# RWKV-7 and a GELU MLP on one core: one TensorE product replaced by block transposes on VectorE, and the first MLP product run in 64x64 tiles

## The chip, the core and the metric

The kernel runs on one core of a Trainium2 chip. The metric is the device time of one execution in microseconds. A core has a matrix engine (TensorE, PE in the profile), VectorE (DVE), ScalarE (ACT), GpSimd (POOL) and SyncE (SP), which here only issues DMAs. Each engine takes its instructions in order, and they wait for each other by semaphores.

## The reference

Everything is in 32-bit floats. A recurrence over 768 tokens runs for 4 batches of 8 heads of dimension 40; its output goes through an MLP of 320 to 2048 to 320 with exact GELU on 3072 tokens.

```python
for t in range(S):
    y[:, :, t] = np.einsum('bhd,bhde->bhe', rt, state)
    Sa = np.einsum('bhde,bhe->bhd', state, at)
    state_decay = state * wt[:, :, None, :] - np.einsum('bhd,bhe->bhde', Sa, bt)
    state = state_decay + np.einsum('bhd,bhe->bhde', vt, kt)
...
h = x @ w_in
g = 0.5 * h * (1.0 + erf(h * inv_sqrt2))
return (g @ w_out)
```

## The kernel before

The tokens are cut into 12 chunks of 64. Within a chunk the recurrence is written as matrix products: the scaled a and b give N (products a.b below the diagonal), whose inverse is needed; k and a give A, v and r give RV. All these 64x64 blocks, one for each of 32 batch-head pairs, are made by `products` (L577) in TensorE tiles of 64 rows by 64 columns, and masked to the upper triangle by VectorE (`masked`, L574).

What a chunk c does, in the order of the loop at L1257:

- `corner` and `joined` (L775, L790) complete the inverse (Tt) from its 32x32 diagonal blocks, with two 32x32 products (J and J2 in the trace). L, which J reads, is Tt turned by VectorE (`turn_corner`).
- `make_X` multiplies the state by a (X) and adds what A and v give (av): xs.
- `make_sa` (L822) multiplies Tt and xs to sa by tokens (tile sap, copied into SM by `copy`); `make_saT` (L834) computes the same product the other way round (saT_ps, copied into saT by two ScalarE copies). So the chunk has sa in both orientations: saT is needed for the product M with r, and sa, which stands beside the masked M in the tile SM, for the last product.
- `make_y2` multiplies r by the turned state into the PSUM tiles QY, `make_M` makes M and masks it into SM, and `make_QY` adds b.SM and k.VR (VR holds v and the masked RV). `outputs` scales QY to the MLP's input xt and to the new state st. `turn_blocks` turns the new state in sixteen 32x32 block steps on VectorE (tile turned).

The inverse of the diagonal blocks is computed two chunks ahead: N is stored to DRAM by SP (`make_N`), read back in another layout (Nb), worked column by column on GpSimd in 62 instructions (L672, L674), stored from GpSimd's queue (inv), and fetched by SP as Tt and T2. The inputs of chunk c+2 are loaded and prepared within chunk c: a, b, k, v and r are read as pairs of rows and turned by VectorE (L186), and the decay w gives the scales wp, en and rw.

The MLP fills TensorE's time. `mlp(c)` (L998) is a generator; each `fill()` in the loop runs it to its next `yield`. A piece of the first product (tile ph) is 20 matmuls of 64x128 weights and 256 columns, in two row tiles side by side, followed by a GELU on ScalarE into gt. From chunk 3 on the second product is computed by `seven` (L947), a seven-product scheme over 2x2 blocks (tile po), whose sums and differences of gt VectorE makes (s1, s2 and the changed blocks of gt). In the steady loop four pieces of ph stand behind X, J2, saT and M of the next chunk, and the po products between the QY pair and the next J.

The order on every engine is the order in which the program issues its instructions (the schedule is manual). PSUM tiles come from a ring of four (`duo`), which is shared by the products and the MLP.

Of the kernel before, what the change touches and what calls it, by code (L numbers as in the profile page):

```python
# [19 lines left out]
def kernel(  # L20
# [464 lines left out]
    def scale_b(c):  # L485
        rwv, wp = decays[c]
        nb = padded[:, c % 2] if c < NB else b_rows[c % 2]
        to = nb[:, :, :, :D] if c < NB else rows(nb)
        nc.vector.scalar_tensor_tensor(to, raws.pop((c, "b")), -1.0, rwv, ALU.mult, ALU.mult)
        turned_in[c]["nb"] = nb  # L490
# [41 lines left out]
    def turn_k(c):  # L532
        t = turned_in[c]
        if c >= NB:
            kT = by_batch(side("k_turned", "conv", 2))
            turn(kT, c, "k_turned")
            en = t.pop("en")
            nc.vector.tensor_tensor(en, kT, en, ALU.mult)
            t["kT"] = parts_by_batch(en)
# [3 lines left out]
        t["kT"] = parts(kT)  # L543

# [80 lines left out]
    def mask_RV(c):  # L625
        t = turned_in[c]
        masked(flat(t["VR"])[:, :, D:], t.pop("RV_ps"))
# [162 lines left out]
    def joined(c):  # L790
# [11 lines left out]
        for q, copy in ((0, nc.scalar.copy), (1, nc.scalar.copy if 0 < c < NS else nc.vector.tensor_copy)):  # L802
# [31 lines left out]
    def make_saT(c):  # L834
# [8 lines left out]
        nc.scalar.copy(to[:, :, 0::3], pt[:, 0])  # L843
        nc.scalar.copy(to[:, :, 1:3], pt[:, 1])
        t["saT"] = parts(saT)

# [24 lines left out]
    def make_QY(c):  # L871
        t = turned_in[c]
        for n, (l_, r_) in enumerate(((t["nb"], t["SM"]), (t["ks"], t["VR"]))):
# [124 lines left out]
    def mlp(c):  # L998
        xt = xts.pop(c)
        for q in range(NF // 4):  # L1000
            ph = duo("ph").rearrange("p x (s t) -> p x s t", s=2)
            for s in range(2):
                p = 2 * q + s
                for kt in range(NK):
                    for x in range(2):
                        nc.tensor.matmul(ph[:, x, s], w_in_sb[half(x), kt, p * P:(p + 1) * P], xt[half(x), kt],  # L1006
                                         start=kt == 0, stop=kt == NK - 1)
            nc.scalar.activation(gt[:, 4 * q:4 * q + 4].rearrange("p (x s) t -> p x s t", x=2), ph, ACT.Gelu)  # L1008
            if c >= NS and q == NF // 4 - 1:
                s1, s2 = half_tile("conv", 2), None  # L1010
                nc.vector.tensor_tensor(s1, block(1, 0), block(1, 1), ALU.add)  # L1011
                if c >= NCH - 2:
                    s2 = half_tile("conv", 2)
                    nc.vector.tensor_tensor(s2, s1, block(0, 0), ALU.subtract)
            yield
        if c >= NS:
            yield from seven(c, s1, s2)
# [239 lines left out]
    for c in range(2, NCH):  # L1257
        n, n2 = c + 1, c + 2
        more, more2 = n < NCH, n2 < NCH
        corner(c)  # L1260
        make_X(c)
        if c > 2:
            turn_blocks(range(4, 16))
        if c == NS + 1:
            weight_sums(3)
        if c == 2:
# [8 lines left out]
            load_v(n)  # L1275
        else:
# [108 lines left out]
```

## Time and profile before

| | us |
|---|---|
| median of three runs | 705.4 (704.87 to 706.5) |
| the profiled execution's own time | 706.29 |
| span of its trace, first to last instruction | 704.3 |
| one period of the chunk loop (J to J) | 49.31 |

In the profile each 32-bit matmul is two records, so 40 records of ph are the 20 matmuls of a piece. PEld is the weight load, which runs beside other matmuls. A row of a timeline gives the start, the duration of the merged group, the engine, line, operation, written and read tiles, shapes and count, and in brackets how long the engine stood idle before it and who released it. SPq rows are DMAs being issued on SP's queue: their duration is that of the issue, not of the transfer.

### The profile page before, as it was taken

The numbers are of one execution on the slowest core, as the hardware profiler recorded it, in microseconds if no ns is written. First come the engines' busy times: TensorE is split into PE (matmuls) and PEld (weight loads), VectorE is DVE, ScalarE is ACT, GpSimd is POOL, SyncE is SP. The second block draws the span as 40 slices with busy tenths as digits, with TensorE's granted clock in tenths as the row PEclk, the third lists the DMA queues.
The fourth block names the chain that finished last, engine by engine and source line by source line (L and its number), as shares of the span: only waits on it lengthen the run. The fifth ranks groups of instructions, "written<-read, shape, count | busy, mean of one in ns | idle before, by whom it ended". The sixth has DMA issues, their size and how long they took to land.

```text
span 704.3 us, 32679 instructions
## 1 busy us (share of the span) xinstructions
PE 662.4 (94%) x14706; PEld 580.0 (82%) x14706; DVE 431.8 (61%) x633; ACT 214.4 (30%) x299; POOL 332.8 (47%) x790
## 2 busy tenths in 40 slices
PE   7588897779999999999999999999999999999997
PEld 4577777657777877889899898998898898998987
DVE  2324889975255666669579488587686694562303
ACT  5124674444131330340341241332323403112020
POOL 5384458810860850871852853835827708600000
PEclk9675799879999999999999999999999999999999
DMA  9688537764665765765666747747758652120100
GB/s 129 120 170 154 103 88 199 136 115 99 118 129 94 125 125 88 130 122 98 125 119 120 140 89 129 139 83 141 138 93 148 126 101 55 37 40 3 35 6 19
DMA packets 287923, 74.45 MB, mean 106 GB/s; under 512 B 265736, under 2 KB 284456, under 8 KB 287784
## 3 DMA queue, kind: packets, MB, share of 16 engines
q1 hardware_dynamic: 283360, 68.20, 52.1%
q0 software_dynamic: 864, 2.36, 2.1%
q8 instruction: 115, 1.88, 1.1%
q10 hardware_dynamic: 3560, 1.80, 1.0%
q14 instruction: 24, 0.20, 0.1%
HBM read 58.69 MB, written 9.70 MB: 97 GB/s over the span
## 4 chain that ended last, share of the span: by engine, by line
PE 77%; DVE 6%; ACT 2%; issue 1%; DMA 1%; ACTq 1%; SPq 0%; DVEq 0%
PE ph L1006 29%; PE po L959 19%; PE po L1023 7%; PE QY L110 6%; PE J L110 2%; PE X L110 2%; PE av L110 2%; PE sap L110 2%; PE saT_ps L110 1%; PE N_ps L110 1%; PE M_ps L110 1%; PE RV_ps L110 1%; PE A_ps L110 1%; PE wT_ps L110 1%; DVE conv L324 1%
## 5 line engine op out<-in xcount | busy, mean ns | idle before, releaser
L1006 PE MATMUL ph<-xt,w_in_sb 64*128 64x256 f32 x1920 | 219.5, 381 | 0.0
L1006 PEld LDWEIGHTS ph<-xt,w_in_sb 64*128 64x128 f32 x1920 | 182.4, 187 | 22.3 <-issue 0.7
L672 POOL TENSOR_TENSOR tmp<-W,Nb 128x126 f32<-128x126 f32 (+22 forms) x310 | 121.5, 392 | 167.0 <-DMA Nb<-N 143.4
L674 POOL TENSOR_TENSOR W<-W,tmp 128x126 f32<-128x126 f32 (+22 forms) x310 | 129.0, 416 | 24.3
L1008 ACT ACTIVATE gt<-ph 128x1024 f32<-128x1024 f32 x48 | 49.1, 1023 | 152.1 <-PE ph L1006 152.0
L959 PE MATMUL po<-w_out_sb,gt 128*128 128x160 f32 x576 | 84.8, 303 | 0.1
L959 PEld LDWEIGHTS po<-w_out_sb,gt 128*128 128x128 f32 x576 | 78.9, 190 | 5.2 <-issue 3.3
L927 DVE STREAM_TRANSPOSE turned<-st 32x256 f32<-32x256 f32 x144 | 62.4, 433 | 2.1
L1023 PE MATMUL po<-w_out_sb,gt 128*128 128x320 f32 x192 | 55.5, 446 | 0.0
L1023 PEld LDWEIGHTS po<-w_out_sb,gt 128*128 128x128 f32 x192 | 36.7, 195 | 15.3 <-issue 1.3
L787 ACT COPY Js<-J 128x256 f32<-128x256 f32 x11 | 4.1, 370 | 95.4 <-PE J L110 95.4
L186 DVE STREAM_TRANSPOSE aT<-a_pairs 128x1024 f32<-128x1024 f32 x9 | 11.2, 1246 | 35.2 <-DMA a_pairs<-in_a_dram 35.2
L1011 DVE TENSOR_TENSOR half<-gt 128x1024 f32<-128x1024 f32 x9 | 11.2, 1247 | 32.8 <-ACT gt L1008 32.8
L575 DVE TENSOR_TENSOR SM<-M_ps,upper 128x1024 f32<-128x1024 f32 x12 | 14.6, 1218 | 23.6 <-PE M_ps L110 23.6
L959 PE MATMUL po<-extra,half 128*128 128x160 f32 x176 | 26.1, 303 | 0.0
L320 ACT ACTIVATE conv<-conv,rebias 128x320 uint32<-128x320 uint32 (+1 forms) x26 | 16.1, 622 | 29.6 <-DVE conv L319 23.2
L959 PEld LDWEIGHTS po<-extra,half 128*128 128x128 f32 x176 | 24.2, 190 | 0.3
L1008 ACT ACT_TABLE_LOAD x10 | 12.8, 1283 | 36.2 <-PE ph L1006 36.1
L963 DVE TENSOR_TENSOR os<-os,po 128x160 f32<-128x160 f32 x36 | 11.5, 319 | 19.0 <-PE po L959 14.3
L575 DVE TENSOR_TENSOR N<-N_ps,upper 128x1024 f32<-128x1024 f32 x12 | 14.7, 1221 | 13.1 <-PE N_ps L110 13.1
L887 DVE TENSOR_TENSOR xt<-QY,wpT 128x512 f32<-128x512 f32 x24 | 15.5, 686 | 11.0 <-PE QY L110 10.9
L662 POOL MEMSET W<- 128x512 f32 x10 | 5.3, 528 | 33.9 <-DMA inv<-W 33.9
(225 smaller groups left out, 1115.6 us busy)
## 6 DMA issues: line engine op xcount, KB each, us to landing
Nb<-N SPq DMA_DIRECT2D x20, 256.0 KB
VR<-in_v_dram SPq DMA_DIRECT2D x24, 160.0 KB
out_dram<-os SPq DMA_DIRECT2D x48, 80.0 KB
b_rows<-in_b_dram SPq DMA_DIRECT2D x22, 160.0 KB
k_rows<-in_k_dram SPq DMA_DIRECT2D x22, 160.0 KB
N<-N SPq DMA_DIRECT2D x44, 64.0 KB
Tt<-inv SPq DMA_DIRECT2D x44, 64.0 KB
a_pairs<-in_a_dram SPq DMA_DIRECT2D x18, 144.0 KB
```

The lines of the kernel that those rows point to most:

```text
L110: nc.tensor.matmul(o, lhsT, rhs, start=first, stop=True, skip_group_check=True)
L320: nc.scalar.activation(power, power, ACT.Relu, bias=rebias, scale=8.0)
L575: nc.vector.tensor_tensor(to, pt, upper.unsqueeze(1).to_broadcast([P, 2 * G * NP, C]), ALU.mult)
L672: eng.tensor_tensor(t, W[:, :rows, j:j + 1].to_broadcast([P, rows, rest]), Nb[:, j:j + 1, j + 1:].to_broadcast([P, rows, rest]), ALU.mult)
L674: eng.tensor_tensor(W[:, :rows, j + 1:], W[:, :rows, j + 1:], t, ALU.add)
L887: nc.vector.tensor_tensor(xt[:, :NP, g * P:(g + 1) * P].rearrange("p i (e t) -> p i e t", e=2), Y, wp[:, g, :, :, :C], ALU.mult)
L927: nc.vector.transpose(tn[to:to + BL, :, at:at + BL], st[at:at + BL, :, g, d * BL:(d + 1) * BL])
L959: nc.tensor.matmul(po[:, n, :DM // 2], l_[:, f], r_[:, f], start=f == 0, stop=f == NF // 2 - 1)
L963: nc.vector.tensor_tensor(to, one_, other, ALU.add)
L1006: nc.tensor.matmul(ph[:, x, s], w_in_sb[half(x), kt, p * P:(p + 1) * P], xt[half(x), kt], start=kt == 0, stop=kt == NK - 1)
L1008: nc.scalar.activation(gt[:, 4 * q:4 * q + 4].rearrange("p (x s) t -> p x s t", x=2), ph, ACT.Gelu)
L1023: nc.tensor.matmul(po[:, g], gt[:, f, g * P:(g + 1) * P], w_out_sb[:, f], start=f == 0, stop=f == NF - 1)
```

## The change

Six things are changed together.

- From chunk 3 on, `make_sa` isn't called. A new function, `sa_blocks`, writes sa by tokens into SM by sixteen 32x32 block transposes of saT on VectorE, twelve behind `make_saT` and four behind `make_M`. Each handles eight blocks. From chunk 4 on the sign of b moves into the copies of saT (now scaled copies on ScalarE).
- A piece of the first MLP product issues 40 matmuls of 64x64 weights instead of 20 of 64x128, in four tiles of the array.
- From chunk 4 on, b and k are scaled by GpSimd (b without the sign), ahead of the inverse's columns, and RV is masked by a ScalarE copy followed by a GpSimd product instead of one VectorE product. For chunk 4 itself the scaling stays on VectorE.
- The turned k is made a chunk later: its transpose stands before the last four state blocks, its scaling with en behind the v transpose.
- Loads are reordered on SP: a is loaded half a chunk earlier, behind the read of Nb; b and k (by rows) are loaded behind the xt copies instead of behind Nb, and the pairs of k behind Nb instead of before xt. The r transpose moves behind that of b.
- s1 and s2 of `seven` are computed at the next fill instead of directly behind the last GELU, and VectorE's copy of J2 is issued ahead of ScalarE's.

The order of PE's products is unchanged except for sap.

```diff
+    def sa_blocks(c, blocks):
+        t = turned_in[c]
+        if "SM" not in t:
+            t["SM"] = SM_ring()
+        saT = t["saT"].rearrange("p q m e t -> p (q m) (e t)")
+        for n in blocks:
+            d, g, e, z = 1 - n // 8, n // 4 % 2, n // 2 % 2, n % 2
+            to, at = e * HP + z * BL, g * HP + d * BL
+            nc.vector.transpose(t["SM"][to:to + BL, g].rearrange("p q m c -> p (q m) c")[:, :, d * BL:(d + 1) * BL],
+                                saT[at:at + BL, :, to:to + BL])
...
-        nc.scalar.copy(to[:, :, 0::3], pt[:, 0])
-        nc.scalar.copy(to[:, :, 1:3], pt[:, 1])
+        sign = 1.0 if c < NB else -1.0
+        nc.scalar.mul(to[:, :, 0::3], pt[:, 0], sign)
+        nc.scalar.mul(to[:, :, 1:3], pt[:, 1], sign)
...
-                    for x in range(2):
-                        nc.tensor.matmul(ph[:, x, s], w_in_sb[half(x), kt, p * P:(p + 1) * P], xt[half(x), kt],
-                                         start=kt == 0, stop=kt == NK - 1)
+                    for to, end in ((0, HP), (HP, P)):
+                        for x in range(2):
+                            nc.tensor.matmul(ph[to:end, x, s], w_in_sb[half(x), kt, p * P + to:p * P + end],
+                                             xt[half(x), kt], start=kt == 0, stop=kt == NK - 1)
...
     def mask_RV(c):
...
+            nc.scalar.copy(to, t.pop("RV_ps"))
+            nc.gpsimd.tensor_tensor(to, to, upper.unsqueeze(1).to_broadcast([P, 2 * G * NP, C]), ALU.mult)
...
+            if more2:
+                turn_a(n2)
+                fetch_pairs(n2, "b_turned", b, nc.sync, False, paired["a"])
+            if more:
+                turn_k(n)
+            if more2:
+                load_r(n2)
+            turn_blocks(range(12, 16))
+            if c == 3:
+                scale_b(n)
+                scale_k(n, nc.vector)
+            fill()
+            make_saT(c)
+            sa_blocks(c, range(12))
         fill()
         make_y2(c)
         make_M(c)
+        if c > 2:
+            sa_blocks(c, range(12, 16))
         if more:
             turn_v(n)
+            if more2:
+                load_v(n2)
+        if more and c > 2:
+            scale_kT(n)
...
         outputs(c)
+        if more2 and c == 2:
+            turn_r(n2)
+            fetch_pairs(n2, "k_turned", k, nc.sync, False, paired["r"])
+        elif more2:
+            load_kb(n2)
         pieces.append(mlp(c))
...
         if more2:
+            if c > 2:
+                scale_b(n2, nc.gpsimd)
+                scale_k(n2, nc.gpsimd)
             steps = start_inverse(n2, nc.gpsimd)
-            load_kb(n2)
+            if more3:
+                load_a(n3)
+            if c == 2:
+                load_kb(n2)
+            else:
+                fetch_pairs(n2, "k_turned", k, nc.sync, False, paired["r"])
             load_VR(n2)
```

More of the change, by code (lines that the diff above doesn't have):

```diff
@@ L801, in joined @@
                     mm(J[lo[q], 0, n // 2], Js[hi[q], n // 2], F[hi[q], n, BL:])
-        for q, copy in ((0, nc.scalar.copy), (1, nc.scalar.copy if 0 < c < NS else nc.vector.tensor_copy)):
+        copies = (0, nc.scalar.copy), (1, nc.scalar.copy if 0 < c < NS else nc.vector.tensor_copy)
+        for q, copy in copies[::-1] if c > 2 else copies:
             copy(F[lo[q], :, BL:].rearrange("p (n z) t -> p z n t", z=2), J[lo[q]])
```

73 lines of the change are left out of this document (36 added, 37 removed).

## The prediction

> **What bounds the kernel now.** I read the page first, then the busy times over one period of the chunk loop, then the chain of work that ended last, then the timelines of the engines over that period.
>
> ```profile
> PE 662.4 (94%) x14706; PEld 580.0 (82%) x14706; DVE 431.8 (61%) x633; ACT 214.4 (30%) x299; POOL 332.8 (47%) x790
> ...
> PEclk9675799879999999999999999999999999999999
> ...
> PE 77%; DVE 6%; ACT 2%; issue 1%; DMA 1%; ACTq 1%; SPq 0%; DVEq 0%
> ```
>
> TensorE is busy for 94% of the span, at 90% or more of full granted clock from a quarter of it on. The next row is one period (from one J product to the next): length, then busy time and instructions of PE, weight loads, DVE, ACT and POOL, then clock, share of the DMA engines and GB/s.
>
> ```profile
> 477.99:527.30 49.31, 49.31 (x1177) 44.70 (x1176) 35.26 (x52) 14.72 (x21) 28.04 (x67) 1.00 0.66 122
> ```
>
> PE has no gap at all in 49.31 us. So a microsecond taken from PE's stream is a microsecond of the period, until another loop becomes longer than PE's. Within PE, the chain shows what a group costs alone and in company (start, us, what):
>
> ```profile
> 588.24 1.07 PE sap L110 x64
> 589.31 1.01 PE saT_ps L110 x62
> 590.33 4.52 PE ph L1006 x40
> 594.84 1.09 PE QY L110 x64
> 595.93 0.93 PE M_ps L110 x64
> ...
> 601.39 3.01 PE QY L110 x128
> ...
> 667.10 17.47 PE ph L1006 x160
> ```
>
> The reader should see two things. Four pieces of the first MLP product (ph) alone between other tile shapes cost 4 x 4.52 = 18.08; four in one run cost 17.47. With a cost u of a piece and s for entering and leaving the run, u + s = 4.52 and 4u + s = 17.47: u = 4.317, s = 0.20. On the other side, the y2 product (first QY row) costs 1.09 and the M product behind it in the same tile shape, with the same count, 0.93: a run of 64x64 products has s = 0.16. So each run of one tile shape costs some 0.18 beside its work.
>
> **The first MLP product in 64x64 tiles.** A piece issues 40 matmuls (80 records, each with a weight load) in place of 20 (40 records), four tiles side by side in place of two. The streamed columns per tile are the same. Does it stream as fast? The QY pair is the row for four tiles with long streams: 128 records in 3.01, less 0.16, over four tiles are 32 steps of 89.1 ns for 104 columns; a ph step now is 4.317/20 = 215.8 ns for 256 columns. Per column that is 0.856 against 0.843 ns.
>
> ```profile
> 460.59 0.74 PE L110 MATMUL cum<-w_tile,cum_m 64*64 64x320 f32 x8
> ...
> 477.99 0.75 PE L110 MATMUL J<-L,N 32*32 32x32 f32 x64
> ...
> 502.61 1.66 PE L110 MATMUL QY<-SM,b_rows 64*64 64x104 f32 x64
> ...
> 518.56 1.16 PE L110 MATMUL N_ps<-aT,nT 40*64 40x64 f32 x64
> ...
> 527.30 0.75 PE L110 MATMUL J<-L,N 32*32 32x32 f32 x64
> ```
>
> The cum row (eight records of 320 columns) confirms four at once: two steps of 320 x 0.843 = 270 ns and a run's 0.2 are 0.74, its duration; with two tiles at a time it would be 1.28. So a piece costs between 4.27 (0.834 ns a column, the slope between the two steps, with nothing fixed) and 4.38 (0.856 x 256). I take 4.32, no change, since that slope with a fixed 2.3 ns fits both rows; the ends are -2 and +3 us over 48 pieces.
>
> The gain is in the runs. From X to QY the loop has the runs X, ph, J2, ph, sap+saT, ph, y2+M, ph, QY: nine. In 64x64 tiles all but J2 (32x32) have one shape and merge: X+ph, J2, and everything behind it: three. Six runs less by 0.18 are 1.08 a chunk, 9.7 over chunks 3 to 11. Chunk 2 (N, ph, sap+saT, ph to one run, ph, y2+M, ph, QY to one) loses six as well: 1.1. Chunks 0 and 1 I count at nothing, because there DVE holds the path:
>
> ```profile
> 114.98 2.36 PE L110 MATMUL QY<-SM,extra 64*64 64x104 f32 x64 [3.60 <-DVE SM L575]
> ```
>
> **sap removed.** Chunks 3 to 11 lose 32 matmuls each: 1.07 less the run's 0.16 is 0.91, nine times 8.2. PE's period becomes 49.31 - 1.08 - 0.91 = 47.32.
>
> **What takes its place on DVE.** Sixteen 32x32 block transposes of saT into SM, of the form of the state's:
>
> ```profile
> 480.74 5.41 DVE L927 STREAM_TRANSPOSE turned<-st 32x256 f32<-32x256 f32 x12
> ...
> 487.94 0.83 DVE L489 SCALAR_TENSOR_TENSOR b_rows<-b_rows,part 128x640 f32<-128x640 f32 x1
> 488.68 1.01 DVE L496 TENSOR_TENSOR k_rows<-k_rows,part 128x640 f32<-128x640 f32 x1
> 490.67 0.83 DVE L832 COPY SM<-sap 128x640 f32<-128x640 f32 x1 [0.98 <-PE sap L110]
> ...
> 498.23 1.22 DVE L575 TENSOR_TENSOR SM<-M_ps,upper 128x1024 f32<-128x1024 f32 x1
> ...
> 519.87 1.22 DVE L575 TENSOR_TENSOR N<-N_ps,upper 128x1024 f32<-128x1024 f32 x1
> 521.00 1.22 DVE L575 TENSOR_TENSOR VR<-RV_ps,upper 128x1024 f32<-128x1024 f32 x1
> 523.24 0.71 DVE L773 STREAM_TRANSPOSE L<-Tt 128x512 f32<-128x512 f32 x1 [1.02 <-DMA Tt<-inv]
> ```
>
> At 5.41/12 = 0.451 each that is 7.2. Gone from DVE are the sap copy, the scalings of b and k and the RV mask, 3.9: DVE goes from 35.3 to 38.6 of 47.3, so its sum does not bind. Its order might. All times here count from the J product (477.99 is zero). ACT turns saT_ps into saT:
>
> ```profile
> 491.73 0.58 ACT L843 COPY saT<-saT_ps 128x512 f32<-128x512 f32 x1 [1.06 <-PE saT_ps L110]
> 492.21 0.59 ACT L844 COPY saT<-saT_ps 128x512 f32<-128x512 f32 x1
> ```
>
> The second copy ends at 14.8 now; sap and two runs earlier that is 13.5 (the copy becomes a scaled copy; I count it the same). Twelve blocks end at 18.9, the M mask (1.22) at 20.1, the last four blocks at 21.9. The QY product with SM starts at 24.62 now, and with the whole saving ahead of it at 22.6. It fits, with 0.7 us to spare, so nothing is lost; the blocks at 0.5 each would use that up.
>
> **POOL and ACT.** The RV mask becomes an ACT copy (some 1 us, ACT is busy 14.7 of 49) and a POOL product of 1024 elements; scaling b and k also goes to POOL. All three stand ahead of the memset and the columns of the inverse.
>
> ```profile
> 481.87 0.24 POOL L672 TENSOR_TENSOR tmp<-W,Nb 128x31 f32<-128x31 f32 x1 [13.32 <-DMA Nb<-N]
> ...
> 512.06 0.23 POOL L674 TENSOR_TENSOR W<-W,tmp 128x16 f32<-128x16 f32 x1
> ...
> 518.36 0.53 POOL L662 MEMSET W<- 128x512 f32 x1 [4.15 <-DMA inv<-W]
> ```
>
> ```profile
> L333 POOL TENSOR_TENSOR w_in_sb<-conv 128x512 f32<-128x512 f32 x7 | 10.0, 1425 | 0.6
> ...
> L496 POOL TENSOR_TENSOR extra<-k_rows,part 128x640 f32<-128x640 f32 x1 | 1.5, 1544 | 1.6 <-DMA k_rows<-in_k_dram 1.6
> ```
>
> Two at 1.54 and one between 1.9 (slope of the two rows) and 2.85 (in proportion), say 2.4, are 5.5. They lie in POOL's 13.32 us wait for Nb: N_ps starts at 40.57 now and 1.99 earlier then; two products on, RV_ps is complete at about 40.5, so the three run from 42 to 47.5, the memsets end by 48.6, and Nb lands at about 52 (below). Without that cover they would cost 5.5 a chunk in the loop below.
>
> **The loop through the inverse.** The N mask of chunk c feeds J two chunks on: N is stored, Nb read, POOL runs the columns, inv is stored, Tt fetched, L turned. On SP's queue:
>
> ```profile
> 478.41 1.36 SPq L163 DMA_DIRECT2D b_rows<-in_b_dram  x2
> 479.87 3.52 SPq L163 DMA_DIRECT2D k_rows<-in_k_dram  x2
> ...
> 509.61 0.85 SPq L895 DMA_DIRECT2D xt<-xt  x1
> ...
> 518.86 1.03 SPq L699 DMA_DIRECT2D Tt<-inv  x2
> 521.11 2.48 SPq L615 DMA_DIRECT2D N<-N  x4
> ...
> 525.91 1.14 SPq L664 DMA_DIRECT2D Nb<-N  x2
> ```
>
> From the N mask's end (521.09) to Nb's last issue (527.05) are 6.0; to the first column, which starts a period after 481.87 at 531.18, 4.1; the columns take 30.4 (481.87 to 512.29); inv's landing 6.1 (to 518.36); Tt's fetch to L's end (523.95) 5.6: 52.2. The mask ends 43.1 behind J, so the loop asks that two periods be at least 95.3; they are 98.6. In the new order a transpose of r (1.2, twice L's 0.71 less the fixed part) stands ahead of the mask, and the stretch starts 2.0 earlier: the mask ends at about 42.4, and the loop asks for 94.6, or 47.3 a period, level with PE's 47.32. So this loop is next, at once.
>
> What can lengthen it is SP. The b and k loads now stand between the xt copies and the Tt fetch, 4.9 us by their rows. Against this the stretch from Nb to xt issues four loads less, and xt starts at 31.6 now because SP, not DVE, is late (the QY pair ended at 27.6); it can start some 3.6 earlier. That leaves Tt late by about 1.3, half of it a period: (94.6 + 1.3)/2 = 47.9, or 0.6 a period over the seven periods where an inverse is waited for: 4 us. The ends are 0 and, with all 4.9 late, 49.7 a period or 17 us.
>
> **The rest.** The a load moves ahead by half a chunk, so DVE's a transpose has less to wait for. s1 moves behind the state update; the po product that needs it comes some 4 us later, which hides its 1.2. The state blocks split 8 + 4 are needed at y2, at 16.6, and are done by 12. The r transpose takes the place on DVE that the RV mask leaves, and its load is issued over 10 us before.
>
> **Sum.** From the profiled execution's own 706.3: 8.2 + 9.7 + 1.1 = 19.0 off, 4 back: 691.3. The median of the runs is 0.9 below that execution, so 690.4; I say 690.
>
> **Rivals.** *The inverse loop takes most of it.* SP's queue issues nearly without a gap, which speaks for it; fewer loads ahead of xt speak against it. 705.4 - 19 + 17 = 703; half of that lateness gives 695.
>
> *The runs cost the same merged.* If the 0.18 is not the change of shape but the change of operands, 10.8 stays: 690 + 11 = 701. Against it: M behind y2 changes operands and is cheaper.
>
> *Slower: the k transpose holds DVE.* It now stands ahead of the SM blocks and waits for a load issued behind Nb and four a loads. Nb's issue ends at about 2.4 in the next period (42.4 + 6.0 + 1.3 - 47.3); eight issues of 0.6 (N: 4 in 2.48) to 1.2 (b and k: 4 in 4.9) and 4.1 to land put it at 11.3 to 16. The k transpose and the last four state blocks take 3.05 and must end by 13.5 plus the 0.7 of QY's margin, so a landing by 11.1 costs nothing; each microsecond later costs eight, one in each of chunks 3 to 10. Past 13 the kernel is slower than before; at 14 it is 690 + 23 = 713. Against it: 65 DMAs are issued in a period of 49.31, 0.76 each with all waits, and the long ones are the b and k rows, which now stand elsewhere.
>
> *Slower: PE's issue binds.* A piece has 80 matmul records and 80 loads. sap's 64 records took 1.07, 16.7 ns each with its load; 80 would take 1.34 of 4.32. It binds from 54 ns a record on and makes the kernel slower than before from 58 ns on (0.32 a piece, 15 over 48); at 64 ns a piece is 5.12 and the time 690 + 38 = 728. The slowest such row here, 2.36 for 64 in chunk 0, is 37 ns, so the rows speak against it. [...]
>
> **How the numbers follow.** Forecast case (683 to 694) 0.58; loop or merged runs at full price (694 to 704) 0.25; k transpose 0.11; issue 0.02; nothing measurable 0.04. A measurement tells about 0.2%, 1.4 us, apart. Faster 0.84, same 0.03, slower 0.13. The low end is the sum without the 4 us of the loop and with pieces at 4.27: 690.4 - 4 - 2.3 = 684, taken as 683; the high end leaves out the slow rivals and the last of the loop's range, together under 2 in 10: 703.
>
> **What would show it.** Right: J to J some 47.5 to 48; ph pieces of 4.3 between saT and y2; no sap. Wrong: PE waiting at J for DVE's L (the loop), at QY for SM (the blocks, and then the k transpose waiting for a load), or ph pieces longer than 4.5.

## The result, and the profile after

The changed kernel takes 697.6 us in the median of four runs (697.5 to 701.4), the kernel before on the same chip 705.95 (704.9 to 708.2): ratio 0.989, 95% interval 0.985 to 0.993. That is 8.4 us less, where 15.4 were forecast. The profiled execution, 701.4, is the longest of the four.

The page of the changed kernel: span, busy times, the queue that brings instructions, and the chain of work that ended last.

```profile
span 699.6 us, 35573 instructions
...
PE 652.4 (93%) x16050; PEld 559.9 (80%) x16050; DVE 465.6 (67%) x746; ACT 222.2 (32%) x307; POOL 386.0 (55%) x812
...
q8 instruction: 126, 2.06, 1.3%
...
PE 61%; SPq 12%; DVE 10%; DMA 7%; POOL 4%; issue 4%; ACT 2%; ACTq 0%; DVEq 0%; POOLq 0%
```

TensorE's share of the chain fell from 77% to 61%; SyncE's queue, VectorE and DMA hold 29% of it. So TensorE no longer sets the end alone. The instruction queue of the kernel before, for comparison:

```profile
q8 instruction: 115, 1.88, 1.1%
```

One period, as for the kernel before (length, then PE, weight loads, DVE, ACT, POOL, then clock, DMA share, GB/s):

```profile
423.88:472.51 48.63, 48.57 (x1273) 43.24 (x1272) 39.29 (x65) 15.68 (x22) 34.33 (x71) 1.00 0.67 124
```

48.63 in place of 49.31, and 47.9 forecast. From J of chunk 5 to J of chunk 11 (six periods) the profiled executions take 293.2 us, before 294.2. Of the 4.7 us between the two spans 1.5 are won up to J of chunk 3, 2.3 in chunk 3, 0.3 in chunk 4, 0.9 in these six periods, and 0.2 are lost at the end.

What the period consists of shows best in groups, each from its start to the next one's start. Where nothing disturbs them they are: J 0.68, X 0.95, first ph piece 4.46, J2 0.68, second 4.37, saT 1.00, third 4.25, y2 and M 1.94, fourth 4.25, QY 3.02, and the rest as before, 21.67: together **47.27 us; the prediction summed 47.32**. The stream itself was forecast rightly. Six periods of it are 281.2 us (the last is shorter by 2.4), so 12.0 us of the 293.2 are something else: 5.0 at the fourth piece and QY, 3.7 in the pieces beside J2, 1.5 at the J of chunk 11, 1.8 in small parts.

The first of these, in the chain of waits of the period that begins at 520.88 (start, us, what):

```profile
530.27 4.20 DMA r_pairs<-in_k_dram
...
534.60 1.42 DVE k_turned L186
536.05 0.43 DVE turned L952
...
537.91 0.43 DVE SM L868
...
543.35 1.22 DVE SM L580
...
545.97 0.45 DVE SM L868
546.46 2.90 PE QY L110 x118
```

The load of k lands 13.6 us behind J; VectorE turns k, then the last state blocks, then the SM blocks, and QY's SM half runs when the sixteenth block is done, 1.6 us late. In the six periods the rows for this wait hold 1.9 us of PE and 2.9 us of weight loads, which overlap. It does not explain all of the 5.0: QY is longer by 1.55, 0.63 and 1.55 us in the periods from 325.36, 423.88 and 520.88 (3.7 together), and by 0.56 and 0.57 in those from 375.24 and 472.51, where SM was in time and a pause of the next kind falls into QY's second half.

The second is in no wait that the profile names; it stands as "issue". The row for ph among the waits of TensorE's weight loads in the six periods, and two groups of its weight loads with such a pause between them:

```profile
PEld ph L1032 <- issue: 4.4, 11, 0.6
```

```profile
332.59 1.06 PEld L1032 LDWEIGHTS ph<-xt,w_in_sb 64*64 64x64 f32 x23
334.21 2.36 PEld L1032 LDWEIGHTS ph<-xt,w_in_sb 64*64 64x64 f32 x48 [0.56 <-issue]
```

Count TensorE's records, that is its matmuls, weight loads and semaphore instructions, together in order of their start. Between the starts of two records inside a product there are, in these six periods, seven gaps of 0.3 us or more and one of 0.298 that no semaphore explains. Each follows a record whose number is 256 n + 192, and ends 1.24 to 1.53 us after a packet of the instruction queue has landed. The rows above fit that: 2.06 MB in 126 packets are 16 KB each (each is 16,384 bytes in the trace), and 32,100 matmuls and weight loads by 126 are 255 a packet. With the semaphore instructions, each of the twenty traces has exactly as many blocks of 256 records, begun at these places, as packets: 126 here, 115 before. **Read together: TensorE's instructions come by DMA here, 256 records to a packet, and when a block is used up before the next is there, TensorE stands.** In all twenty traces no block's first record started sooner than 1.16 us after its packet had landed (1.24 in the changed kernel's, 1.33 in the one before). The packet's transfer takes 1.1 us and begins, in the middle, 0.9 us (before) or 1.2 us (after) after TensorE entered the block ahead, in the loop at most 3.0 (2.69 and 2.30 in these two; runs 14 to 16 below aside): by these figures, as an estimate, a block must last some 3.2 to 5.3 us (0.9 to 3.0, with 1.1 and 1.16).

Before, a piece of ph was 80 records in 4.5 us and stretched each block. Now it is 160, and J, X and J2 have 128 each, before as now, in 0.7 to 0.95 us. A block of J's end, X and half a piece lasts 3.3 us. Worse, a period now has 2562 records, ten blocks and 2, so the begins of blocks stay where they are in the loop: 83, 339, 595 records behind J and so on, falling by 2 a period. Worked out from the records (us of pause at each place; a step of ph alone is 0.2):

```
J at     339 (ph 1)  595 (ph 2)  1363 (ph 4)  1619 (QY)
325.4    0.45        0.48        0.01         0.00
375.2    0.21        0.26        0.00         0.33
423.9    0.02        0.21        0.31         0.00
472.5    0.15        0.00        0.06         0.32
520.9    0.49        0.22        0.00         0.00
571.0    0.30        0.48        0.00         0.03
```

Before, a period had 2367 records and the places wandered by 63 a period; 3 blocks of 55 came within 1.75 us of their packet, now 25 of 59.

A pause costs more than its own length. In the period from 423.88 it is 0.02 us in the first piece, yet the piece takes 4.69: behind the begin of the block the four tiles no longer start together, and at the end of the piece three of the last four matmuls start together and one 0.22 us later. With that, the pieces beside J2 lose the 3.7 us and QY 1.1 of the 12.0.

### The profile page after: what moved, and what is told of

It is laid out like the page before. It is cut to its first block, busy times and chain, and to the rows that moved or that the text cites. A ratio compares the mean times of both kernels' runs of the same rounds, so it can differ in the third digit from the quotient of the medians.

```text
span 699.6 us, 35573 instructions
## 1 busy us (share of the span) xinstructions
PE 652.4 (93%) x16050; PEld 559.9 (80%) x16050; DVE 465.6 (67%) x746; ACT 222.2 (32%) x307; POOL 386.0 (55%) x812
## 3 DMA queue, kind: packets, MB, share of 16 engines
q8 instruction: 126, 2.06, 1.3%
## 4 chain that ended last, share of the span: by engine, by line
PE 61%; SPq 12%; DVE 10%; DMA 7%; POOL 4%; issue 4%; ACT 2%; ACTq 0%; DVEq 0%; POOLq 0%
PE ph L1032 18%; PE po L984 14%; PE po L1048 7%; PE QY L110 5%; DVE SM L868 3%; SPq L163 3%; DMA VR<-in_v_dram 3%; SPq L181 2%; POOL tmp L682 2%; SPq L709 2%; POOL W L684 2%; DMA r_pairs<-in_k_dram 2%; PE sq L110 2%; PE J L110 2%; PE N_ps L110 2%
## 5 line engine op out<-in xcount | busy, mean ns | idle before, releaser
L1032 PE MATMUL ph<-xt,w_in_sb 64*64 64x256 f32 x3840 | 227.8, 380 | 2.7 <-issue 1.5
L1032 PEld LDWEIGHTS ph<-xt,w_in_sb 64*64 64x64 f32 x3840 | 171.4, 134 | 41.2 <-issue 9.3
L682 POOL TENSOR_TENSOR tmp<-W,Nb 128x126 f32<-128x126 f32 (+22 forms) x310 | 129.2, 417 | 103.0 <-DMA Nb<-N 79.5
L684 POOL TENSOR_TENSOR W<-W,tmp 128x126 f32<-128x126 f32 (+22 forms) x310 | 134.7, 434 | 24.3
L868 DVE STREAM_TRANSPOSE SM<-saT 32x256 f32<-32x256 f32 x144 | 62.8, 436 | 9.9 <-ACT saT L856 7.4
L637 POOL TENSOR_TENSOR VR<-VR,upper 128x1024 f32<-128x1024 f32 x8 | 18.9, 2368 | 34.1 <-ACT VR L636 34.1
L783 DVE STREAM_TRANSPOSE L<-Tt 128x512 f32<-128x512 f32 x11 | 7.8, 710 | 35.9 <-DMA Tt<-inv 35.9
L912 DVE TENSOR_TENSOR xt<-QY,wpT 128x512 f32<-128x512 f32 x24 | 15.4, 686 | 16.1 <-PE QY L110 15.9
L580 DVE TENSOR_TENSOR N<-N_ps,upper 128x1024 f32<-128x1024 f32 x12 | 14.6, 1219 | 11.1 <-PE N_ps L110 11.1
L984 PE MATMUL po<-extra,gt 128*128 128x160 f32 x144 | 21.0, 299 | 0.0
```

Source lines behind the costliest of these rows:

```text
L637: nc.gpsimd.tensor_tensor(to, to, upper.unsqueeze(1).to_broadcast([P, 2 * G * NP, C]), ALU.mult)
L682: eng.tensor_tensor(t, W[:, :rows, j:j + 1].to_broadcast([P, rows, rest]), Nb[:, j:j + 1, j + 1:].to_broadcast([P, rows, rest]), ALU.mult)
L684: eng.tensor_tensor(W[:, :rows, j + 1:], W[:, :rows, j + 1:], t, ALU.add)
L868: nc.vector.transpose(t["SM"][to:to + BL, g].rearrange("p q m c -> p (q m) c")[:, :, d * BL:(d + 1) * BL], saT[at:at + BL, :, to:to + BL])
L984: nc.tensor.matmul(po[:, n, :DM // 2], l_[:, f], r_[:, f], start=f == 0, stop=f == NF // 2 - 1)
L1032: nc.tensor.matmul(ph[to:end, x, s], w_in_sb[half(x), kt, p * P + to:p * P + end], xt[half(x), kt], start=kt == 0, stop=kt == NK - 1)
```

## The experiments

"J5 to J11" below is the time from J of chunk 5 to J of chunk 11 in the run's trace (six periods), "pauses" the sum of the gaps at begins of blocks in it (an estimate: gaps of 0.3 us and more alone are 2.9 us in the changed kernel, 0.8 before, 14.8 in run 10 and 1.6 in run 13), "half clock" the time in it at half the granted clock. They say more than the totals: runs of one kernel on one chip spread over up to 16 us, and in the traces the J of chunk 5 stands anywhere between 322 and 333 us.

```
kernel                              ratio to before  95%              J5-J11  pauses  half clock
before                                                                294.2   0.5     0
after                               0.989            0.985 to 0.993   293.2   4.4     0
1  tiles only                       0.997            0.995 to 1.000   294.9   6.9     0
2  order only                       0.992            0.990 to 0.995   290.2   0.3     0
3  half the tiles                   0.991            0.988 to 0.995   294.1   4.4     3.4
4  k behind                         1.017            1.014 to 1.020   311.6   0.6     30.7
5  after again                      0.994            0.991 to 0.998   294.4   5.5     3.4
6  state blocks first               0.996            0.992 to 0.999   296.7   5.8     6.8
7  6 with half the tiles            0.999            0.996 to 1.002   295.1   5.3     3.4
8  6 without pair loads             0.981            0.977 to 0.986   288.1   4.8     0
9  after, 176 records ahead         1.000            0.997 to 1.004   293.6   6.5     3.4
10 after, 28 records ahead          0.999            0.995 to 1.002   298.5   15.2    0
13 after, 228 records ahead         0.994            0.990 to 0.997   288.8   2.7     0
17 6 and 13                         1.003            1.000 to 1.006   295.3   5.5     0
18 17 without pair loads            0.993            0.990 to 0.995   290.3   8.0     0
```

**1 and 2, the two halves of the change.** The kernel before with the new loop of the ph product alone; and the changed kernel with the old one:

```diff
-                    for to, end in ((0, HP), (HP, P)):
-                        for x in range(2):
-                            nc.tensor.matmul(ph[to:end, x, s], ...
+                    for x in range(2):
+                        nc.tensor.matmul(ph[:, x, s], ...
```

> The kernel before with only the first MLP product in 64x64 tiles; sap, the old order of loads and the old work of VectorE stay. If merged runs save 0.18 us each (the step of the prediction): 1.08 a chunk, 706.0 - 10.8 = 695. If the merged runs themselves save little: the ph pieces between two 64x64 products stay above 4.4 us and the time is 702 to 706. If TensorE's supply of instructions is what fails (a piece is now 160 records and not 80, loads included): the pieces on both sides of J2 show single holes of 0.2 to 0.5 us inside a run of ph, as in the changed kernel (4.68 and 4.69 us, where the piece behind saT has 4.15), some 0.7 a chunk, and the time is 699 to 701. If those holes come from the new order of the loads instead, the pieces on both sides of J2 are at 4.2 to 4.4 here.

> The changed kernel with the first MLP product back in 64x128 tiles (two side by side): sap is gone, the blocks of SM, the new order of loads and GpSimd's work stay. By the prediction's steps: 706.0 - 8.2 = 697.8, a period of 48.4 us. If VectorE's order behind the k transpose holds QY (theory: lost at QY), the wait at QY for SM costs up to 1 us a chunk, and the time is 699 to 705; TensorE being slower here, the wait should be shorter than in the changed kernel, so that 698 to 700 is my figure. If the supply of instructions costs the changed kernel 0.7 a chunk, no hole appears in the ph pieces here: each 4.5.

By the ratio, the tiles alone bring 1.8 us of their forecast 10.8. Their runs do merge (ph pieces of 4.25 to 4.46 where nothing stops them, and 4.52 in 23 of 24 pieces of run 2), but pauses of up to 1.6 us take it back. In TensorE's timeline of run 1 a piece broken in the middle, with the wait for which no releaser is found:

```profile
387.40 0.74 PE L1007 MATMUL ph<-xt,w_in_sb 64*64 64x256 f32 x7
388.90 0.88 PE L1007 MATMUL ph<-xt,w_in_sb 64*64 64x256 f32 x12 [0.76 <-issue]
...
442.78 0.81 PE L110 MATMUL M_ps<-rT,saT 40*64 40x64 f32 x40
444.51 0.28 PE L110 MATMUL M_ps<-rT,saT 40*64 40x64 f32 x4 [0.92 <-issue]
```

Since run 1 has the old order of loads, the new order is not what makes the pauses. The order alone brings 5.4 us of 8.2, and its period is within 0.03 of what the sum said (49.31 - 0.91):

```profile
420.31:468.68 48.37, 48.37 (x1114) 43.76 (x1113) 38.74 (x62) 15.75 (x22) 33.88 (x71) 1.00 0.68 124
```

**3, 64x64 tiles for the third and fourth piece only** (`((0, HP), (HP, P)) if q > 1 else ((0, P),)`).

> The changed kernel, with 64x64 tiles only for the third and fourth piece of each first MLP product (between saT, y2, M and QY), and 64x128 for the two pieces on both sides of J2. Two changes of shape come back (X to ph, ph to saT) at 0.18 each: by merged runs alone 0.36 a chunk, 10 chunks, 3.6 us and 1 for the last chunks: 701 to 702. If the supply of instructions is what costs the pieces beside J2 (4.68 and 4.69 instead of some 4.3), those go back to 4.5 and the time stays at 697 to 698.5.

Undecided: the pieces beside J2 are at 4.52 in ten cases of twelve, but pauses of the same sum, 4.4 us, come elsewhere (M, po, X), since the places of the blocks move with the number of records.

**4, the transpose of k behind the SM blocks**, and the r load that takes its buffer with it:

```diff
-            if more:
-                turn_k(n)
-            if more2:
-                load_r(n2)
             turn_blocks(range(12, 16))
 ...
             sa_blocks(c, range(12, 16))
+            if more:
+                turn_k(n)
+            if more2:
+                load_r(n2)
```

> The changed kernel with the transpose of k, and the r load that waits for its buffer, moved behind the last four SM blocks on VectorE, so that the blocks wait for no load of k. If the transpose of k holding VectorE ahead of the blocks is what costs time at QY (0.3 to 1.4 us a chunk in the trace of the changed kernel), the wait at QY for SM goes and the time falls by 3 to 7 us, to 691 to 694. If the missing time lies in the ph pieces beside J2 (supply of instructions), it falls by 0 to 2: 695.5 to 697.5. If the later r load, and what stands behind it on SP's queue, comes late for v, the xt copies or Tt, it is above 698.

12 us slower than the kernel before and nearly 20 than the changed one, by its third case. QY no longer waits (3.02 in four of six periods), but SyncE stands at the load of r until k is turned at 457.4 and issues everything behind it later; Tt and L are late for the J of chunks 5 to 10. SyncE's and VectorE's timelines, and the waits of the whole trace:

```profile
457.41 5.01 SPq L178 DMA_DIRECT2D r_pairs<-in_r_dram  x8
...
484.81 0.71 DVE L783 STREAM_TRANSPOSE L<-Tt 128x512 f32<-128x512 f32 x1 [7.79 <-DMA Tt<-inv]
```

```profile
PE J L110 <- DVE L L783: 20.7, 8, 3.6
```

And each such wait is paid for twice: 3.4 or 6.8 us at half clock follow it, 30.7 us in the loop.

**5, 6 and 7: the changed kernel again; with the last four state blocks ahead of the transposes of a and k** (`turn_blocks(range(12, 16))` moved in front of `turn_a(n2)`); **and that with half the tiles.**

> The changed kernel once more, as the base for the other three runs on this chip. Expected 697 to 701 us. In its trace TensorE should again pause only at every 256th of its records (matmuls and weight loads counted together, the 192nd of each 256), each time resuming 1.2 to 1.7 us after a 16 KB transfer of instructions ended (theory: supply of instructions), some 4 us in all over six periods; and QY should wait for SM some 0.8 us a period (theory: VectorE's order).

> The changed kernel with the last four state blocks (1.8 us of VectorE) moved ahead of the transposes of a and k, into the time in which VectorE waits for those loads (1.6 and 1.1 us). If VectorE's order behind the k load is what QY waits for, the SM blocks start 1 to 1.8 us earlier, the wait at QY goes in nearly all chunks, and the time falls by 0.8 a chunk over eight chunks: 691 to 694 where the base has 697.5. If QY's wait comes from elsewhere (saT later than I think, or the M product), the time stays within 1.5 us of the base. Pauses at the instruction blocks stay as they are, 0.6 to 0.75 a period.

> As the run with the state blocks moved, and with 64x64 tiles only for the third and fourth piece of each first MLP product (64x128 on both sides of J2). By merged runs alone it loses 0.36 a chunk against that run, some 4 us. If TensorE's supply of instructions fails where J, X and J2 (128 records in 0.7 to 0.95 us each) stand beside pieces of 160 records, it wins 0.4 to 0.7 a chunk back: 0 to 3 us faster than that run.

Run 5 has its pauses at the same places (0.3 to 1.05 us at 329 to 339 and 585 to 595, in eight of twelve cases), but not the wait at QY: its rows for SM hold 0.5 and 0.7 us in six periods, in one of them, where 0.8 a period was expected. So that wait differs much between executions. Run 6 hardly has it, and wins nothing. TensorE's waits over the six periods, first of the changed kernel, then of run 6 (us in total, times, longest):

```profile
PEld QY L110 <- DVE SM L868: 2.9, 5, 0.7
PE QY L110 <- DVE SM L868: 1.9, 4, 0.5
```

```profile
PE J L110 <- DVE L L783: 2.7, 2, 2.2
...
PEld QY L110 <- DVE SM L868: 0.4, 1, 0.4
...
PE QY L110 <- DVE SM L868: 0.2, 1, 0.2
```

The wait for SM is all but gone, but against run 5 on the same chip that is little. QY still takes 3.58 to 3.86 us in five of the six periods: in four of them a block begins in its second half, with a gap of 0.27 to 0.65 us. The wait for L, 1.4 us in the changed kernel at the J of chunk 11 and 2.1 in run 5, is 2.7: the inverse's loop, which the prediction had level with TensorE, is near. In run 5 one such wait shows its second price, in TensorE's timeline and in a window behind it:

```profile
475.88 0.74 PE L110 MATMUL J<-L,N 32*32 32x32 f32 x64 [1.74 <-DVE L L783]
```

```profile
477.50:481.10 3.60, 3.60 (x51) 2.32 (x47) 3.39 (x9) 0.00 (x0) 0.00 (x0) 0.53 0.87 191
```

After 1.74 us of waiting the granted clock is at a half for 3.4 us, and the ph piece there takes 6.14 us, not 4.46. Run 7 settles nothing that run 3 left open.

**8 and 18: loads left out** from chunk 6 on (`for x in range(2 if c < 6 else 0)` in the pair loads), once as run 6, once as run 17.

> As the run with the state blocks moved; from chunk 6 on it leaves out the loads of a, b, r, k and v (the transposes then read older data); w, the rows of b and k, the stores and the inverse's transfers stay. With nothing late for VectorE and SP's queue short, the period from the fifth chunk on shows TensorE's stream alone: 47.3 us by the prediction's sum. If the pauses at the instruction blocks come only from queueing behind the loads (the transfer of a block starts some 1.2 us after TensorE crossed into the block before), the start comes at once and the pauses go: 47.3. If the way of a block alone (1.1 us of transfer and 1.2 to 1.5 us until its first use) is too long for 256 records here, pauses of 0.1 to 0.5 us stay and the period is 47.5 to 47.9. If the runs' own cost or the pieces were mis-sized, the period is above 48 with no pause at a block.

> The same, and from chunk 6 on it leaves out the loads of a, b, r, k and v (the transposes read older data). With the same loads left out and no added records, J to J was 47.9 to 49.2, and all of what was above 47.4 lay at the begins of blocks in the first ph piece. Theory of the supply: with the blocks moved these pauses fall to 0 to 0.3 us a period, and J to J is 47.3 to 47.6, the prediction's sum for TensorE's stream (47.32). If the first piece still takes 5 us and more, something else than the place of the blocks holds it.

With no load late, QY is 3.0 to 3.1 in eleven of twelve periods, and there is no wait for SM and none for L of over 0.25 us. What is left above 47.3 is the first and second piece: in run 18 the period from 381.95 is 48.63 with a first piece of 5.81; take its excess over 4.46 off and 47.28 remain. So the sum holds. The pauses did not go, though run 18 was expected to lose them: its first piece takes over 5.5 us in each period, the sign put down for a cause other than the place of the blocks. The long gaps are still at the begins of blocks. With the pair loads gone, Nb, VR and the stores of the output move together behind J, and the packets for that place begin 2.2 to 2.7 us after TensorE entered the block ahead (1.0 to 1.2 in run 13). That what else is moving delays a packet, and that leaving loads out only changed what that is, is likely, not shown.

**9, 10 and 13: the same kernel with the blocks shifted.** Products of ones, used by nothing, at the very start (44, 7 and 57 of them, four records each):

```diff
         mm(pt[:, n % 2], w_in_sb[:, 0, :P], w_in_sb[:, 0, :512])
+    for n in range(44):
+        mm(pt[:BL, n % 2, :BL], w_in_sb[:BL, 0, :BL], w_in_sb[:BL, 0, :BL])
```

> The changed kernel with 44 further 32x32 products of ones (176 records of TensorE, under 2 us of it at the very start, used by nothing) behind the first warm-up products. The loop of the changed kernel issues 2562 records a period, ten times 256 and 2, so the places where a new block of 256 records begins stay nearly fixed in the loop: 73 to 83 records behind J's first, and every 256 from there. The added records move them to about 3. Theory of the supply: the blocks that begin with J (J and X, 256 records in 1.6 us) and with y2 and M (256 in 2.05 us) are used up long before the next, some 3.7 us away, is there; pauses of about 2 us behind X and 1.5 us in M come in each period, in place of the 0.6 to 0.75 us now: J to J 50 to 51, and the time 10 to 25 us above the run with 28 records, more where a pause of over 1.5 us brings the half clock. If the alignment does not matter (queueing of loads, or TensorE's own issue), the time is within 3 us of that run.

> The changed kernel with 7 further such products (28 records) at the start: the blocks begin some 110 records behind J. There no block is used up in less than 3.3 us by the records of the traces without pauses, and the pauses should fall to 0.3 to 0.5 us a period: 0 to 3 us faster than the changed kernel on the same chip. If alignment does not matter: the same time as the changed kernel and as the run with 176 records.

> The changed kernel with 57 further 32x32 products (228 records of TensorE) at the start. Records added ahead of the loop push J later in its block of 256, so the place of the next block's begin behind J falls: from 73 to 83 by 228 to 101 to 111 (counted modulo 256). In the stretches without pauses, no block that begins there is used up in under 3.3 us; the two runs with 176 and 28 records had blocks of 2.1 and 2.65 us and pauses of 1.5 us at just those ends. Theory of the supply: pauses of 0.2 to 0.5 us a period (0.75 in the changed kernel, 2.65 with 28 records), J to J 48 to 48.5 us where nothing else is late. If the places are chance, pauses at the pieces beside J2 stay at 0.6 or more a period.

For 9 and 10 I had the sign wrong: records ahead push J later in its block, so the places fall, by 176 to 163 and by 28 to 55 (counted modulo 256). By that rule the shortest block in run 9 ends in RV, and in run 10 in the first piece. Just there the pauses are, in TensorE's timelines of run 9 and of run 10:

```profile
372.94 1.11 PE L110 MATMUL RV_ps<-rT,vT 40*64 40x64 f32 x64
373.98 0.40 PE L984 MATMUL po<-w_out_sb,gt 128*128 128x160 f32 x1
375.56 2.60 PE L984 MATMUL po<-w_out_sb,gt 128*128 128x160 f32 x18 [1.18 <-issue]
...
383.67 4.53 PE L1032 MATMUL ph<-xt,w_in_sb 64*64 64x256 f32 x80
```

```profile
374.21 1.92 PE L1032 MATMUL ph<-xt,w_in_sb 64*64 64x256 f32 x26
377.41 1.99 PE L1032 MATMUL ph<-xt,w_in_sb 64*64 64x256 f32 x31 [1.28 <-issue]
```

In run 9 the first and second piece are 4.46 and 4.37 in all six periods, and 0.7 to 1.5 us are lost behind RV, 2467 records from J, in five of six. In run 10 the pauses are 0.6 to 2.2 us at records 301 to 311 and 0.5 to 0.85 at about 1330, 15.2 in all. In run 13 they are 2.7, less than in the changed kernel (4.4 and 5.5). Nothing but 28, 176 or 228 records at the very start was added: the alignment alone is worth up to 10 us in six periods (288.8 against 298.5), while two traces of the changed kernel itself are 1.2 apart (293.2 and 294.4). That is shown. The run times do not show it (0.999, 1.000, 0.994): each trace is one execution, and the stretch before the loop differs by up to 11 us between them.

**17: both remedies.**

> The changed kernel with the 228 records at the start and the last four state blocks ahead of the transposes of a and k: both on SyncE's old queue order. In the run with the 228 records alone the pieces beside J2 were at 4.46 and 4.4 us nearly throughout, and QY stood at 3.0 to 4.55 for 3.02 because of SM, some 4 us over six periods; the state blocks moved took that wait from 1.9 us to 0.2 in their run. If the two causes add, J to J is 47.5 to 47.9 (48.5 with the records alone) and the time 4 to 6 us under the run with the records alone: 698 to 700 by medians on that chip, with the fastest runs near 690. If removing them only uncovers the inverse's loop, a wait for L at J of 1 to 2 us appears in one or two periods, with 3.4 us of half clock, and the time stays within 2 us.

Its second case, though without half clock up to the last J. The wait for SM is down to 0.5 us of PE and 1.0 of weight loads, and J waits for L five times, the J of chunk 11 included, 5.9 us in all, on top of pauses of 5.5:

```profile
525.00 0.71 DVE L783 STREAM_TRANSPOSE L<-Tt 128x512 f32<-128x512 f32 x1 [5.73 <-DMA Tt<-inv]
```

```profile
525.85 0.74 PE L110 MATMUL J<-L,N 32*32 32x32 f32 x64 [1.60 <-DVE L L783]
```

**11, 12, 14, 15 and 16: other queues for the inverse.** N's stores and Nb's loads on ScalarE's queue (11; 12 with 64x128 tiles); Tt and T2 on it (14; 15 with 228 records; 16 with 64x128 tiles), all with the state blocks first.

> The changed kernel with the last four state blocks ahead of the transposes of a and k, and with the stores of N and the loads of Nb issued on ScalarE's queue (idle from the copy of RV to the copy of Js) in place of SyncE's. SyncE then fetches all of Tt at once and reaches the loads of a and k some 4 us earlier. If SyncE's queue is what makes L late for J (1.4 to 2.3 us in single periods, each followed by 3.4 us at half clock) and k late for VectorE: no wait for L at J in chunks 3 to 10, SM blocks 1 us earlier, and the time 3 to 7 us under the changed kernel's. If N's way by ScalarE comes later than by SyncE, POOL's first column is later and the time the same or up to 4 us worse.

> As the run with N on ScalarE's queue, with the first MLP product back in 64x128 tiles throughout. TensorE has 2242 records a period in place of 2562, and its blocks of 256 move through the loop by 62 a period, so that a bad place comes now and then only: pauses of 0.1 us a period in place of 0.7. Its stream alone is 48.37 us a period, 1.1 above the tiles of 64x64. If pauses, and the half clock behind them, cost more than the merged runs win: 694 to 698, below the run before. Otherwise it is 4 to 8 us above it.

> The changed kernel with the last four state blocks ahead of the transposes of a and k, and with all fetches of the inverse (Tt and T2) issued on ScalarE's queue behind the copy of RV, where ScalarE has nothing to do until J is done. On SyncE's queue N's store and Nb's load then no longer stand behind a fetch that waits for the inverse to land (up to 5 us in the runs before), and the loads of a and k start 1 to 3 us earlier. If that coupling is what makes L late for J in single periods: no wait for L in chunks 3 to 10, no half clock there, 2 to 6 us under the changed kernel. If L is late because POOL starts late for other reasons, the wait stays at 1.5 to 2.5 us in one or two periods and the time is the same.

> Both together: the inverse fetched by ScalarE, the state blocks first, and the 228 records ahead. If the three causes (blocks of instructions, VectorE ahead of QY, the inverse's loop) are all there is between the forecast and the measurement, J to J comes to 47.5 to 48 and the time to 690 to 694 on a chip where the kernel before has 705.5. If each remedy only uncovers the next wait, it stays within 2 us of the run with the 228 records alone.

> As the run with the inverse fetched by ScalarE, with the first MLP product in 64x128 tiles throughout (no added records). TensorE's stream alone is 48.37 us a period, and with nothing late and blocks that wander through the loop: 48.4 to 48.5, 698 us. If the 64x64 tiles are worth their 1.1 us a period once nothing else is late, this is 6 to 8 us above the run with both remedies; if the pauses eat the gain, it is level with it or below.

All five miss: 751, 773, 781, 790 and 780 us, ratios 1.07 to 1.12. SyncE's and ScalarE's queues are not independent in this program: the traces show the same eight completion counters on both (semaphores 101 and 104 to 110 in the kernel before and the changed one), and a transfer is issued only when the one that had its counter before it, on whichever queue, is done. In the changed kernel's trace all 16 landings of the first lie between the two issues in 704 of the 754 pairs of successive transfers on one counter; 24 of the 754 go from one queue to the other. In run 14 SyncE's copies of xt stood from 434.2 until the fetches on ScalarE had been issued, at 451.2:

```profile
433.38 0.83 SPq L920 DMA_DIRECT2D xt<-xt  x1
451.22 2.52 SPq L923 DMA_DIRECT2D xt<-xt  x4
```

So they say nothing about the inverse's loop with a lighter SyncE queue; that stays open. No run that does all of the work beat the changed kernel by more than the spread.

## Why the prediction was right and wrong

The three signs of being wrong that the prediction named are all in the trace: J waits for L, QY waits for SM behind a late k load, and pieces of ph are longer than 4.5 us. The measured time lies in the case that had 0.25, but the two causes named for that case are not what brought it there: the loop took little, and the merged runs do cost less.

- **Direction and stream: right.** Merged runs, pieces that stream as fast in 64x64 tiles, sap gone: the undisturbed groups sum to 47.27 us a period (47.32 forecast), and to 48.37 without the tiles (47.32 + 1.08 is 48.40).
- **"PE issue binds" was weighed by the wrong quantity; this is the step that failed.** It asked for the rate of a record, found 16.7 ns against a bound of 54, and gave it 0.02. The rate is indeed no bound: J's 64 matmul records and as many loads take 0.68 us, an undisturbed piece 4.25 to 4.46, and no run shows the issue of a record taking the 54, 58 or 64 ns of its slow case. The supply, for which the sum has no term, is: by the estimate above 256 records have to last 3.2 us and more, and the tiles doubled ph's records just beside J, X and J2. The rows for it, the instruction queue's packets and the count of records in a period, were on the page before and were not read. Measured: 4.4 us of pauses in six periods, 0.7 a period (0.8 by what the pieces and QY lose), where nothing was put down; with tiles alone 6.9, which is nearly all of what the tiles win.
- **"It fits, with 0.7 us to spare": wrong, by the k load.** The prediction had that as a slow rival: landing past 11.1 us behind J costs a microsecond for each. The k load landed 10.6 to 13.6 us behind J in the six periods, which by the rival costs 7.1 us; QY lost 3.7 us to it, 0.6 a period, and in run 5 about 0.2 a period. That the pieces' own pauses gave VectorE time is likely (in run 5, with longer ones, the wait is shorter), not shown. It was not slower than before, as the rival would have it from 13 us on.
- **The inverse's loop: put down at too much, but near.** 0.6 us a period was put down; the changed kernel loses 1.5 us at one J, 0.25 a period. It is close to TensorE's period, as the sum said: in run 17, with the wait for SM small, J waits 5.9 us in all, and holding SyncE's r load back in run 4 brings out 17.4.
- **A price that was in no term: the clock.** A wait of 1.7 us at J in run 5 was followed by 3.4 us at half clock, another 1.7 us. The stretches here are 3.4 us long or a multiple (3.41, 6.83, 13.65 and 27.31 us in the changed kernel's trace, 1.28 at its very end), and in run 4 their starts are 51.2 or 54.6 us apart, 15 or 16 times 3.41. In the runs of the table the waits ahead of them were mostly shorter than 3.4 us: from 0.6 us (run 3) to 3.6 (run 4).
- **POOL, right.** RV's product takes 2.37 us (2.4 estimated), and POOL still waits for Nb, 79.5 us in all where it was 143.4: the cover held.
- **Chunk 2: mis-sized to the good side.** Its period is 2.1 us shorter, 1.1 forecast; but the stretch before the loop differs by more than that between executions.

So of 7.6 us between forecast and measurement, pauses of instruction blocks are worth some 0.8 us a period in the profiled execution, VectorE ahead of QY 0.6 and the loop 0.25, together more than the 0.6 kept for the loop. How the three share the medians is open: no run that does all of the work removed them all.

## What to carry to other kernels

Count TensorE's records, weight loads included, in every stretch of 256: here, by the estimate above, the instruction supply could stop TensorE where they were used up in under 3.2 to 5.3 us, and 64x64 tiles doubled those of a ph piece, from 80 to 160. A number of records per period near a multiple of 256 (2562 here) kept the bad places where they were in the loop; 7 to 57 idle products at the start moved them (runs 9, 10 and 13). Before taking a wait away, ask which loop is level behind it, and price a wait with the half clock that may follow (3.4 us of it behind 1.7 us of waiting in run 5, behind 0.6 in run 3).

## What the runs showed of the hardware

- TensorE's records and the packets of the instruction queue go together: as many blocks of 256 records as packets of 16 KB (126 in the changed kernel, 115 before; so in all twenty traces). A packet's transfer takes 1.1 us in the middle and begins, in the middle, 1.2 us (0.9 before) after TensorE entered the block ahead; first use never sooner than 1.16 us after it.
- In the loop half clock came in stretches of 3.4 us or multiples, and within 4 us of waits or pauses of 0.6 to 3.6 us (1.4 in the changed kernel, 1.7 in run 5, 2.2 in run 6), though not after every one: waits at J of 1.1 to 1.6 us in run 17, and pauses in ph of 1.6 us in runs 1 and 8 and 2.2 in run 10, were not followed by it. So no length of wait from which it comes is shown; the 1.5 us in the expectation of run 9 was the author's estimate.
- At half clock a step of four 64x64 ph tiles takes 427 ns (changed kernel, 621.9 to 625.3) for 216 (at 440.5).
